# Scores one tile further ahead of the product with the values, and the queries split earlier, in a pooled-attention and maxout kernel

## The chip, the cores and the metric

The kernel runs on one core of a Trainium2 chip. The metric is the device time of one execution in microseconds. The engines are TensorE (PE in the profile, its weight loads PEld), VectorE (DVE), ScalarE (ACT), GpSimd (POOL) and SyncE (SP), which issues the DMAs.

## The reference

The keys and values are one tensor: a 4 x 4 mean of `kv` times a small matrix. The attention over 768 pooled positions is followed by a feed-forward part (FFN) with three matrices and a maximum.

```python
kv_pool = kv.reshape(B, H // r, r, W // r, r, C).mean(axis=(2, 4))      # r = 4
k = v = kv_pool.reshape(B, -1, C) @ w_sr                                # 4 x 768 x 128
s = scale * (q @ k.transpose(0, 2, 1))                                  # q: 4 x 12288 x 128
a = np.exp(s - s.max(-1, keepdims=True))
a /= a.sum(-1, keepdims=True) + 1e-09
x = (a @ v).reshape(B * N, C)
h = np.maximum(np.maximum(x @ w1, x @ w2), x @ w3)                      # 768 columns
return (h @ w_out).astype(np.float32)
```

## The kernel before

**Groups, tiles, steps.** The 49152 queries are worked through in 96 groups of 512 (24 to each batch). A group has four score tiles of 128 queries. The main loop at the end of the kernel runs over the groups g, and in each over six FFN steps f = 0 to 5, one for every 128 of the 768 hidden columns; n = 6 g + f counts them. While the FFN of group g runs, the scores of later groups, the product with the values of group g + 1, and the keys of the next batch are worked in between.

**The order.** What stands on each engine's queue is written out by hand: `ORDER` (L160) has twelve strings of tokens, the first six for the steps of an even group, the others for an odd one. `step` (L973) carries the tokens out one after the other, and every engine works its instructions in this order. The tokens that matter here:

- H: six matmuls into two banks ps_h (two buffers). R: ScalarE's Relu of the first bank. M: VectorE's h, the maximum of that with the second bank, which frees it.
- C: ScalarE's half-precision cast hh of h. L: GpSimd's remainder hl = h - hh. O: the product of the step two before with w_out, into ps_o; for f = 0 of a group it begins a new ps_o, of which there is one buffer.
- S: the six score matmuls of the next tile, into ps_s. m: VectorE's maximum mx and the bias nb. e: ScalarE's exponential a. c: ScalarE's cast ahl. l: GpSimd's remainder ahl, and a DMA that turns both halves into aT (two buffers, one per group).
- X: half of the product of aT with the values (ps_x) for group g + 1, at f = 1 and f = 4; for the first two groups both halves at f = 4. xh, xl: the halves of this product, at f = 5.
- P: VectorE copies the finished ps_o to o_planes, and a DMA turns it. G: VectorE's merge of what came back (o_sb<-o_turned). T: rs and the scaling (o_sb<-o_sb,w_down,rs), and the store.
- qd, qc, qp: once or twice per pair of groups, the load of 1024 queries, GpSimd's scaling of their columns, and VectorE's largest value with the scale q_up and q_sc. qh and ql: the two halves of 512 queries each; ScalarE casts q_hl from q_sb and q_up, VectorE makes the remainder q_hl, and a DMA turns both into qT (four buffers).
- k: a piece of the next batch's keys (`keys_step`, L1068). In groups 3 to 8 of a batch VectorE adds pieces of kv at f = 0, 2, 3 and 4 (odd groups) or sums them (even ones); groups 9 to 14 find the largest value, transpose and project.

**When a tile is scored.** Until group 1, `FIRST` says how many tiles S takes at each step; 13 are taken by its end, so it is one tile ahead of the three groups 1 to 3. From group 2 on S takes a tile at f = 0, 2, 3 and 5. So the last tile of group g + 2 is scored at f = 3 of group g, and X of that group begins at f = 1 of group g + 1. Between the score and its l lie two more steps: a tile scored at f = 3 is sent off by l at f = 0 of the next group, a tile scored at f = 2 at f = 4.

The queries of groups 2 p + 4 and 2 p + 5 are split (qh, ql) at f = 3 and f = 4 of the odd group 2 p + 1; ql stands behind M there.

Of the kernel before, what the change touches and what calls it, by code (L numbers as in the profile page):

```python
# [20 lines left out]
def kernel(  # L21
# [32 lines left out]
    B, N, C = q.shape  # L54
    _, HH, WW, _ = kv.shape
    R = 4
# [5 lines left out]
    NFT = DF // P  # L62
    G = 512
# [59 lines left out]
    def times(t, src, by, by2=None):  # L123
# [27 lines left out]
    FIRST = (1, 1, 2, 2, 0, 1, 1, 1, 1, 2, 0, 1)  # L151
    JOIN_ON_POOL, LO_ON_DVE, HI_ON_DVE, HL_ON_DVE = ((0, 2, 6), (3,), (6, 8), ())
    OUT_AT, OUT_ON = (1, 8), ("dve", "dve")
    ATTEND = {0: (4, 4), 1: (4, 4)}
    LATE = (1,)
    LOADS = (('k01', 'k00', 'k02', 'k03', 'q', 'k10', 'k11', 'k12', 'k13', 'k22', 'k20', 'k21', 'k23', 'w00', 'w10'), ('w20',), ('w01', 'w21', 'w11'))
    WEIGHTS = {(0, 0): (10, 12, 15, 18, 20, 21), (1, 0): (19, 20, 20, 20, 21, 21, 22), (2, 0): (21, 21, 21, 21, 21, 22, 22), (0, 1): (22, 22, 22, 23, 23, 23), (1, 1): (22, 23, 24, 24, 24, 24, 25), (2, 1): (24, 24, 25, 25, 25, 25, 25), (3, 0): (25, 25, 26, 26, 26, 26, 27), (3, 1): (26, 26, 26, 27, 27, 27, 27)}
    SIZE = {22: 0, 25: 1, 27: 2}
# [14 lines left out]
    )  # L173
    OUTS = {2: (), 3: (), 4: (0, 1, 2)}
# [141 lines left out]
    class Keys:  # L316
# [19 lines left out]
        def load(self, s, i):  # L336
            piece = kvp.tile([P, PIECE], F32, name="kv_piece")
            src = kv[self.b].rearrange("(s h i) (w r) c -> s i h w (r c)", s=KS, i=R, w=KW)
            sp_dma.dma_start(out=piece, in_=src[s, i])
            self.pieces[s, i] = piece  # L340
# [107 lines left out]
        def project(self, h):  # L448
            mm(
                out=self.spare()[:, :HALF], lhsT=wsr_sb, rhs=self.poolT[:, h * HALF:(h + 1) * HALF],  # L450
                start=True, stop=True,
            )
# [33 lines left out]
    def q_peak(s):  # L486

        assert s < 2 or next_q["cols"] >= 2 * s + 2
        row = qp.tile([P, 1], F32, name="q_row", bufs=2)
        dve.tensor_reduce(out=row, in_=st["q"][s], axis=AX.XY, op=ALU.max, apply_absolute_value=True)  # L490
        up = qp.tile([P, 1], F32, name="q_up", bufs=2)
        dve.tensor_scalar(
            out=row.bitcast(I32), in0=row.bitcast(I32), scalar1=EXPO, scalar2=None, op0=ALU.bitwise_and
        )
        dve.tensor_scalar(out=up, in0=row, scalar1=TINY, scalar2=2.0 ** -14, op0=ALU.max, op1=ALU.mult)
        dve.reciprocal(out=up, in_=up)
        st["qr"][s] = (row, up)
# [84 lines left out]
    def soft_max(g, j):  # L582
        mx = tiny.tile([P, 1], F32, name="mx")
        dve.tensor_reduce(out=mx, in_=st["ps"][g, j], axis=AX.XY, op=ALU.max, negate=True)
        soft_bias(g, j, mx)
# [76 lines left out]
    def hidden(g, f):  # L662
        xh, xl = st["x"][g]
        assert not st["hp"]
        fh, fs = f // (NFT // 2), slice(f % (NFT // 2) * P, (f % (NFT // 2) + 1) * P)
        for i in range(2):
            p = ps_h.tile([P, G], F32, name="ps_h")
            mm(out=p, lhsT=d_hi[i][fh][:, fs], rhs=xh, start=True, stop=False)
            mm(out=p, lhsT=d_lo[i][fh][:, fs], rhs=xh, start=False, stop=False)
            mm(out=p, lhsT=d_hi[i][fh][:, fs], rhs=xl, start=False, stop=True)  # L670
            st["hp"][i] = p

    def hidden_first():
        h1 = hp.tile([P, G], F32, name="h1", bufs=2)
        act.activation(out=h1, in_=st["hp"].pop(0), func=AF.Relu, scale=H_DOWN)
        return h1

    def hidden_max(h1):
        h = hp.tile([P, G], F32, name="h", bufs=4)
        dve.scalar_tensor_tensor(  # L680
            out=h, in0=st["hp"].pop(1), scalar=H_DOWN, in1=h1, op0=ALU.mult, op1=ALU.max
        )
        return h

    def hidden_hi(g, f):
        hh = hp.tile([P, G], F16, name="hh", bufs=HB_)
        act.copy(out=hh, in_=st["h"][g, f])
        st["h"][g, f] = (st["h"][g, f], hh)

    def hidden_lo(g, f):  # L690
        h, hh = st["h"][g, f]
        hl = hp.tile([P, G], F16, name="hl", bufs=HB_)
        (dve if g * NFT + f in HL_ON_DVE else pool).tensor_tensor(out=hl, in0=h, in1=hh, op=ALU.subtract)
        st["h"][g, f] = (hh, hl)
# [129 lines left out]
    k = KT[0] = Keys(0)  # L824
# [19 lines left out]
    def loads(n):  # L844
        for what in LOADS[n]:
            load(what)
# [98 lines left out]
    def late(n):  # L945
        if n == LATE[0]:
            q_peak(1)
            q_exps(1)
            q_split(2)
        weights(23 + n)  # L950
        if n in (1, 2):
            turn_w1(n - 1)
        if n == 5:
            product_w1()
# [14 lines left out]
    def drain(queue):  # L969
        while queue:  # L970
            yield queue.pop(0)

    def step(token, g, f):  # L973

        n = g * NFT + f
        if token == "H":
            hidden(g, f)
            to_relu.append((g, f))
        elif token == "R":
            for gf in drain(to_relu):  # L980
                to_h.append((gf, hidden_first()))
        elif token == "M":
            for gf, h1 in drain(to_h):
                st["h"][gf] = hidden_max(h1)
                to_hh.append(gf)
        elif token == "C":
            for gf in drain(to_hh):
                hidden_hi(*gf)
                to_hl.append(gf)
        elif token == "L":  # L990
            for gf in drain(to_hl):
                hidden_lo(*gf)
        elif token == "O":
            if g < 2:
                late(n)
            for m in OUTS.get(n, (n - 2,)):
                if m >= 0:
                    project(*divmod(m, NFT))
        elif token == "S":
            for _ in range(FIRST[n] if g < 2 else f not in (1, 4)):  # L1000
                if tiles:
                    to_max.append(tiles.pop(0))
                    scores(*to_max[-1])
        elif token == "X":
            for part, slot in enumerate(ATTEND.get(g, (1, 4))):
                if f == slot and g < NG - 1:
                    attend(g + 1, part)
        elif token == "m":
            for t in drain(to_max):
                soft_max(*t)  # L1010
                to_exp.append(t)
        elif token == "e":
            for t in drain(to_exp):
                soft_exp(*t)
                to_hi.append(t)
        elif token == "c":
            for t in drain(to_hi):
                soft_hi(*t)
                to_lo.append(t)
        elif token == "l":  # L1020
            for t in drain(to_lo):
                soft_lo(*t)
        elif token == "xh":
            if g + 1 < NG:
                attended_hi(g + 1)
        elif token == "xl":
            if g + 1 < NG:
                attended_lo(g + 1)
        elif token == "P":
            if g > 0:  # L1030
                turn_out(g - 1)
                to_merge.append((g - 1, n))
        elif token in ("G", "T"):
            if token == "G":
                while to_merge and (to_merge[0][1] < n - 1 or g == NG - 1 and f == NFT - 2):
                    m = to_merge.pop(0)[0]
                    merge(m)
                    to_scale.append(m)
            else:
                for m in drain(to_scale):  # L1040
                    scale_out(m, finish_scale(m))
        elif token == "qd":
            s = turn("load", NG // 2)
            if s:
                q_load(s)
        elif token == "qc":
            q = turn("cols", NG)
            if q:
                q_cols(q)
        elif token == "qp":  # L1050
            s = turn("peak", NG // 2)
            if s:
                q_peak(s)
                q_exps(s)
        elif token == "qh":
            q = turn("hi", NG)
            if q:
                q_hi(q)
        elif token == "ql":
            q = turn("lo", NG)  # L1060
            if q:
                q_lo(q)
        elif token == "k":
            keys_step(g, f)
        else:
            raise ValueError(token)
# [94 lines left out]
```

## Time and profile before

| | |
|---|---|
| time, median of 3 runs (lowest to highest) | 2059.89 us (2055.98 to 2059.9) |
| span of the profiled execution (its only time) | 2060.3 us |
| DVE q_hl, all of them | 96, 72.0 us |
| DVE h, all of them | 575, 396.5 us |
| DVE o_planes, all of them | 95, 115.9 us |
| POOL hl and ahl | 670.1 and 627.2 us |
| aT, median from issue to landing | 4.0 us |
| qT, median from issue to landing | 3.1 us |

An engine's share of busy time is over the whole span, of which the first 150 us are the start (weights, first keys). Matmuls overlap: each is drawn longer than the distance to the next one, so sums of their durations are larger than the time that they take. Nearly every line has the number of one helper, L103, so the groups are told apart by tiles. A row of the time line shows the start, the length, the engine, and what is written from what, and in brackets the idle time before it with what ended it.

### The profile page before, as it was taken

Reading aid. Unit: us, or ns where it says so; the run is one execution under the profiler, and the core shown is the slowest. Engines: PE = TensorE matmul, PEld = TensorE weight load, DVE = VectorE, ACT = ScalarE, POOL = GpSimd, SP = SyncE. Lnnn points to the kernel's source line nnn. Section 1 sums busy time; section 2 is a strip of 40 time slices with the busy share of each in tenths; the row PEclk is TensorE's granted clock in tenths of the full one; section 3 lists DMA queues with packets and bytes.
Section 4 is the critical chain, followed back from the end, with each engine's and each line's share of the span. In section 5 each row is a group of like instructions: output and inputs, shape, how many; then the busy total and the mean of one; then the engine's idle time right before and its main releaser. Section 6 shows DMA issues by size and latency. Waiting matters only on the chain.

```text
span 2060.3 us, 29166 instructions
## 1 busy us (share of the span) xinstructions
PE 1981.9 (96%) x9797; PEld 967.2 (47%) x9797; DVE 1510.4 (73%) x2482; ACT 1457.4 (71%) x2535; POOL 1409.2 (68%) x1064
## 2 busy tenths in 40 slices
PE   6489999999999999999999999999999999999998
PEld 5244444444444444444444444444444444444444
DVE  5767886677777887777777788677776777777775
ACT  2367777777777777777777777677777777777774
POOL 2257677777777767677776777677777776767764
PEclk8699999999999999999999999999999999999999
DMA  8177766667668876666667786757666676666662
GB/s 255 29 141 167 168 139 128 129 127 141 135 125 171 185 153 126 125 143 127 130 132 161 161 184 131 135 121 133 133 133 127 126 139 131 126 132 142 120 121 68
DMA packets 839959, 283.30 MB, mean 138 GB/s; under 512 B 813440, under 2 KB 814592, under 8 KB 839808
## 3 DMA queue, kind: packets, MB, share of 16 engines
q1 hardware_dynamic: 839808, 281.43, 66.5%
q8 instruction: 77, 1.26, 0.3%
q14 instruction: 74, 0.61, 0.1%
HBM read 53.54 MB, written 25.17 MB: 38 GB/s over the span
## 4 chain that ended last, share of the span: by engine, by line
PE 78%; DVE 8%; ACT 5%; DMA 5%; issue 2%; POOL 2%; SPq 0%; DVEq 0%; ACTq 0%; POOLq 0%
PE ps_h L103 30%; PE ps_o L103 17%; PE ps_x L103 16%; PE ps_s L103 15%; DMA aT<-ahl 4%; DVE h L103 1%; ACT ahl L103 1%; DVE kv_piece L103 1%; DVE q_row L103 1%; ACT a L103 1%; POOL ahl L103 1%; DVE mx L103 1%; ACT hh L103 1%; ACT xh L103 1%; ACT h L103 1%
## 5 line engine op out<-in xcount | busy, mean ns | idle before, releaser
L103 POOL TENSOR_TENSOR ahl<-a,ahl 128x768 f16<-128x768 f32 x383 | 627.2, 1648 | 321.9 <-issue 180.1
L103 POOL TENSOR_TENSOR hl<-h,hh 128x512 f16<-128x512 f32 x575 | 670.1, 1176 | 205.1 <-ACT hh L103 204.8
L103 DVE SCALAR_TENSOR_TENSOR h<-ps_h,h 128x512 f32<-128x512 f32 x575 | 396.5, 690 | 186.4 <-ACT h L103 90.5
L103 ACT ACTIVATE h<-ps_h 128x512 f32<-128x512 f32 x575 | 341.7, 594 | 243.7 <-PE ps_h L103 240.4
L103 ACT CAST hh<-h 128x512 f16<-128x512 f32 x577 | 349.8, 615 | 167.6 <-DVE h L103 167.4
L103 DVE TENSOR_REDUCE mx<-ps_s 128x1 f32<-128x768 f32 x383 | 365.4, 954 | 112.4 <-PE ps_s L103 111.9
L103 PE MATMUL ps_h<-xh,d_hi 128*128 128x512 f16 x1150 | 437.7, 381 | 7.6 <-ACT w1T L103 5.9
L103 PE MATMUL ps_h<-xh,d_lo 128*128 128x512 f16 x1150 | 437.7, 381 | 0.0
L103 PE MATMUL ps_h<-xl,d_hi 128*128 128x512 f16 x1150 | 437.6, 380 | 0.0
L103 ACT ACTIVATE a<-ps_s,nb,q_sc 128x768 f32<-128x768 f32 x383 | 377.4, 988 | 56.4 <-DVE nb L103 51.1
L103 PE MATMUL ps_x<-aT,v_hi 128*128 128x512 f16 (+1 forms) x1188 | 377.0, 376 | 22.5 <-DMA aT<-ahl 21.2
L103 PE MATMUL ps_s<-k_hi,qT 128*128 128x384 f16 x1532 | 376.3, 328 | 4.0 <-ACT a L103 3.3
L103 PEld LDWEIGHTS <-d_hi 128*128 128x128 f16 x2308 | 226.2, 98 | 258.8 <-issue 2.8
L103 PE MATMUL ps_o<-hh,wo 128*128 128x512 f16 x1140 | 340.5, 381 | 2.3 <-DVE wo L103 2.3
L103 PEld LDWEIGHTS <-qT 128*128 128x128 f16 x2304 | 226.7, 98 | 197.0 <-issue 10.1
L103 ACT CAST ahl<-a 128x768 f16<-128x768 f32 x382 | 312.4, 832 | 4.6 <-DMA aT<-ahl 0.2
L103 PEld LDWEIGHTS <-wo 128*128 128x128 f16 x1710 | 167.6, 98 | 195.1 <-DVE wo L103 2.3
L103 PE MATMUL ps_s<-k_lo,qT 128*128 128x384 f16 x766 | 251.5, 328 | 0.3 <-DVE k_lo L103 0.3
L103 PE MATMUL ps_x<-aT,v_lo 128*128 128x512 f16 (+1 forms) x594 | 222.7, 376 | 0.0
L103 PE MATMUL ps_o<-hl,wo 128*128 128x512 f16 x570 | 216.9, 380 | 0.0
L103 POOL TENSOR_TENSOR q_sb<-q_sb,col_row 128x512 f32<-128x512 f32 x96 | 126.2, 1315 | 101.4 <-DMA q_sb<-in_q_dram 91.4
L103 PEld LDWEIGHTS <-v_hi 128*128 128x128 f16 x1188 | 116.8, 99 | 149.7 <-DMA aT<-ahl 9.6
(148 smaller groups left out, 1425.8 us busy)
## 6 DMA issues: line engine op xcount, KB each, us to landing
kv_piece<-in_kv_dram SPq DMA_DIRECT2D x48, 512.0 KB, 5.0
q_sb<-in_q_dram SPq DMA_DIRECT2D x48, 512.0 KB, 4.5
out_dram<-o_sb SPq DMA_DIRECT2D x95, 256.0 KB, 2.2
aT<-ahl SPq DMA_TRANSPOSE x384, 4.0
kv_piece<-in_moe_w_dram SPq DMA_DIRECT2D x6, 384.0 KB, 5.6
qT<-q_hl SPq DMA_TRANSPOSE x96, 3.1
o_turned<-o_planes SPq DMA_TRANSPOSE x95, 3.3
kv_piece<-in_moe_w_out_dram SPq DMA_DIRECT2D x2, 384.0 KB, 3.8
```

Source lines behind the costliest of these rows:

```text
L103: return lambda **kw: tc.keep_in_program_order(op(**kw))
```

## The change

It adds one number and a condition: in group 2, S also takes a tile at f = 4 (n = 16). From then on every tile is scored one place earlier: the last tile of a group at f = 2 instead of f = 3, the first at f = 3 of the group before instead of f = 5. In the loop over S's places the tile that would have been taken last of all leaves its place empty. The tokens qh and ql leave f = 3 and f = 4 of the odd groups and come to f = 0 and f = 1; qh stands ahead of R, and ql behind M and behind k.

```diff
+    AHEAD = 2 * NFT + 4
...
     ORDER = (
...
-        "H C m l R M e k c L X O S",
-        "H C G R l L O m M c S k X e",
+        "H C m qh l R M e k c ql L X O S",
+        "H C G qh R l L O m M c S k ql X e",
         "H l P L k C R T e M m O S X c",
-        "H L C qh R m M l X O S e k ql c",
-        "H L m qh R l M c e X S O k C ql",
+        "H L C R m M l X O S e k c",
+        "H L m R l M c e X S O k C",
         "H xh m C L xl l c e R M O S X k qd",
     )
...
         elif token == "S":
-            for _ in range(FIRST[n] if g < 2 else f not in (1, 4)):
+            for _ in range(FIRST[n] if g < 2 else f not in (1, 4) or n == AHEAD):
```

On VectorE, in the odd group 69 from its maximum at f = 0 (the first row) to the h of f = 2 (the last), there stood before:

```order
L103 TENSOR_REDUCE mx<-ps_s 128x1
L103 TENSOR_SCALAR nb<-mx,q_sc 128x1
L103 SCALAR_TENSOR_TENSOR h<-ps_h,h_17048 128x512
L103 COPY o_sb<-o_turned 128x2x512
L103 TENSOR_REDUCE mx<-ps_s 128x1
L103 TENSOR_SCALAR nb<-mx,q_sc 128x1
L103 SCALAR_TENSOR_TENSOR h<-ps_h,h_17081 128x512
L103 COPY o_planes<-ps_o 128x1024
L103 TENSOR_SCALAR rs<-sm,o_down 128x4
L103 RECIPROCAL rs<-rs 128x4
L103 SCALAR_TENSOR_TENSOR o_sb<-o_sb,w_down,rs 128x512
L103 SCALAR_TENSOR_TENSOR h<-ps_h,h_17126 128x512
```

At the same place, from the h of f = 0 (the first row) on, there stands now:

```order
L103 SCALAR_TENSOR_TENSOR h<-ps_h,h_17069 128x512
L103 SCALAR_TENSOR_TENSOR q_hl<-q_sb,q_up,q_hl 128x4x128
L103 COPY o_sb<-o_turned 128x2x512
L103 TENSOR_REDUCE mx<-ps_s 128x1
L103 TENSOR_SCALAR nb<-mx,q_sc 128x1
L103 SCALAR_TENSOR_TENSOR h<-ps_h,h_17106 128x512
L103 SCALAR_TENSOR_TENSOR q_hl<-q_sb,q_up,q_hl 128x4x128
L103 COPY o_planes<-ps_o 128x1024
L103 TENSOR_SCALAR rs<-sm,o_down 128x4
L103 RECIPROCAL rs<-rs 128x4
L103 SCALAR_TENSOR_TENSOR o_sb<-o_sb,w_down,rs 128x512
L103 SCALAR_TENSOR_TENSOR h<-ps_h,h_17153 128x512
```

A q_hl has come behind each of the first two h, the second of them directly ahead of o_planes.

On ScalarE, from the cast hh at f = 0 of the same group (the first row) to the cast ahead of f = 2's Relu, there stood before:

```order
L103 CAST hh<-h 128x512
L103 ACTIVATE h_17048<-ps_h 128x512
L103 ACTIVATE a,sm<-ps_s,nb,q_sc 128x768
L103 CAST ahl<-a 128x768
L103 CAST hh<-h 128x512
L103 ACTIVATE h_17081<-ps_h 128x512
L103 ACTIVATE a,sm<-ps_s,nb,q_sc 128x768
L103 CAST hh<-h 128x512
```

And there stands now:

```order
L103 CAST hh<-h 128x512
L103 ACTIVATE q_hl<-q_sb,q_up 128x4x128
L103 ACTIVATE h_17069<-ps_h 128x512
L103 ACTIVATE a,sm<-ps_s,nb,q_sc 128x768
L103 CAST ahl<-a 128x768
L103 CAST hh<-h 128x512
L103 ACTIVATE q_hl<-q_sb,q_up 128x4x128
L103 ACTIVATE h_17106<-ps_h 128x512
L103 ACTIVATE a,sm<-ps_s,nb,q_sc 128x768
L103 CAST hh<-h 128x512
```

Each Relu (h from ps_h) of f = 0 and f = 1 now has a q_hl ahead of it. TensorE's queue differs in two places only: six score matmuls come in at step n = 16, and the last place of S, far down, is empty.

## The prediction

> **What bounds the kernel now.** I read the page's head first, then the table of stretches, then TensorE's waits after the start-up, which name what interrupts it.
>
> ```profile
> span 2060.3 us, 29166 instructions
> PE 1981.9 (96%) x9797; PEld 967.2 (47%) x9797; DVE 1510.4 (73%) x2482; ACT 1457.4 (71%) x2535; POOL 1409.2 (68%) x1064
> ```
>
> Stretches: length, then busy time of PE, PEld, DVE, ACT, POOL, and the granted clock.
>
> ```profile
> 400.00:600.00 200.00, 200.00 (x988) 96.43 (x987) 144.60 (x234) 148.95 (x259) 144.60 (x110) 1.00 0.67 133
> ```
>
> TensorE's waits from 150 us to the end: total us, times, longest.
>
> ```profile
> PE ps_x L103 <- DMA aT<-ahl: 12.6, 15, 2.3
> PE ps_x L103 <- DVE pool_max L103: 3.4, 3, 1.1
> PE ps_x L103 <- issue: 1.3, 2, 0.7
> ```
>
> TensorE bounds the steady part: 200.00 of 200 us busy at clock 1.00. The number of matmuls does not change, so only its waits can be won, and any new wait is lost in full. What is there to win is the product with the values (ps_x) waiting for the turned exponentials (aT), 12.6 us, and the two "issue" waits at the same product, 1.3 us.
>
> **What the change removes.** A recorded wait is short by a little. TensorE in order of time: start, length, instruction, [idle before it]:
>
> ```profile
> 151.66 0.39 PE L103 MATMUL ps_x<-aT,v_hi 128*128 128x512 f16 x1 [0.72 <-DMA aT<-ahl]
> ...
> 726.55 0.39 PE L103 MATMUL ps_x<-aT,v_hi 128*128 128x512 f16 x1 [1.81 <-DMA aT<-ahl]
> ...
> 1525.00 0.38 PE L103 MATMUL ps_h<-xh,d_hi 128*128 128x512 f16 x1
> 1525.22 0.38 PE L103 MATMUL ps_h<-xh,d_lo 128*128 128x512 f16 x1
> ...
> 1526.30 0.60 PE L103 MATMUL ps_o<-hh,wo 128*128 128x512 f16 x2
> ...
> 1527.92 0.38 PE L103 MATMUL ps_h<-xh,d_hi 128*128 128x512 f16 x1
> ```
>
> A matmul is drawn 0.38 us long, but its successor starts 0.22 us after it, so each wait costs 0.16 us more than is written. 17 waits make 13.9 + 17 x 0.16 = 16.6 us. One of them, 0.72 + 0.16 us at 151.66, belongs to group 3, whose tiles keep their places. So about **16 us** can go. I take all of it: the longest wait is 2.3 us, and a group's last tile is now split into halves and sent off two steps earlier (scored at f=2 and split at f=4, instead of f=3 and the next group's f=0); a step is 2.9 us (1525.00 to 1527.92) or more. The new overlap on the two aT buffers costs nothing: the first tile of group g+2 takes the buffer of group g, and ScalarE casts that tile behind the xh of group g, which itself waits for the product that frees the buffer. PE's only reordered instructions are one tile's six score matmuls at step 16, once: I cost them at nothing (one exponential is 0.99 us; up to that if they wait).
>
> **What the change moves.** Per pair of groups, two ScalarE casts (q_hl, hi) and two VectorE instructions (q_hl, lo) with their two transposes go from f=3 and f=4 of the odd group to f=0 and f=1. The transposes on SP go ahead of o_turned; each queued there follows its own producer, the SP queue is not what PE waits for, and qT is needed at f=3 only: nothing. What matters is VectorE. Here are the odd steps of a pair without key work (group 69): VectorE, then ScalarE, then GpSimd, in order of time.
>
> ```profile
> 1518.46 0.16 DVE L103 RECIPROCAL q_up<-q_up 128x1 f32<-128x1 f32 x1
> ...
> 1519.76 0.68 DVE L103 SCALAR_TENSOR_TENSOR h<-ps_h,h 128x512 f32<-128x512 f32 x1
> ...
> 1522.99 0.69 DVE L103 SCALAR_TENSOR_TENSOR h<-ps_h,h 128x512 f32<-128x512 f32 x1 [0.80 <-ACT h L103]
> 1523.60 1.22 DVE L103 COPY o_planes<-ps_o 128x1024 uint16<-128x1024 uint16 x1
> ...
> 1526.84 0.68 DVE L103 SCALAR_TENSOR_TENSOR h<-ps_h,h 128x512 f32<-128x512 f32 x1
> ```
>
> ```profile
> 1521.79 0.61 ACT L103 CAST hh<-h 128x512 f16<-128x512 f32 x1
> 1522.31 0.59 ACT L103 ACTIVATE h<-ps_h 128x512 f32<-128x512 f32 x1
> ...
> 1528.08 0.72 ACT L103 ACTIVATE q_hl<-q_sb,q_up 128x512 f16<-128x512 f32 x1
> 1528.77 0.60 ACT L103 ACTIVATE h<-ps_h 128x512 f32<-128x512 f32 x1
> ```
>
> ```profile
> 1523.62 2.28 POOL L103 TENSOR_TENSOR hl<-h,hh 128x512 f16<-128x512 f32 x2
> ```
>
> Step f=0: the first cast waits for q_up (1518.62), and its successor starts 0.69 us behind it (1528.08 to 1528.77), so the Relu h ends near 1519.97 and VectorE's h starts at 1520.06 instead of 1519.76. TensorE next writes that bank at 1521.1: hidden.
>
> Step f=1: the second cast takes the Relu's place at 1522.31; the Relu moves 0.69 us, and VectorE's h from 1522.99 to 1523.68 (the first q_hl and the merge o_sb fit into the 0.80 us in which VectorE waited). Then the second q_hl stands ahead of o_planes. It would start at 1524.28, and at that time GpSimd works on hl (1523.62 to 1524.78). What that means is shown by the same form of instruction elsewhere:
>
> ```profile
> 402.88 1.31 DVE L103 SCALAR_TENSOR_TENSOR o_sb<-o_sb,w_down,rs 128x512 f32<-128x512 f32 x1
> ...
> 1526.17 0.75 DVE L103 SCALAR_TENSOR_TENSOR o_sb<-o_sb,w_down,rs 128x512 f32<-128x512 f32 x1
> ```
>
> ```profile
> 402.45 1.20 POOL L103 TENSOR_TENSOR hl<-h,hh 128x512 f16<-128x512 f32 x1 [0.58 <-ACT hh L103]
> ```
>
> And VectorE's group of all q_hl: busy us, mean ns of one, then idle before:
>
> ```profile
> L103 DVE SCALAR_TENSOR_TENSOR q_hl<-q_sb,q_up,q_hl 128x512 f16<-128x512 f32 x96 | 72.0, 750 | 4.8 <-ACT q_hl L103 4.8
> ```
>
> Started inside a GpSimd instruction, o_sb took 1.31 us and ended 0.54 us after it (404.19 against 403.65); started outside, 0.75. The trace has no q_hl inside one: its mean of 750 ns over 96 is the undisturbed time. So its price here is between 0.74 us and, as o_sb paid, the end of hl plus 0.55: 1525.33. I take the latter, since the two have the same form and two SBUF inputs. o_planes then runs 1525.25 to 1526.47 instead of 1523.60 to 1524.82.
>
> The Trainium skill, page "SBUF — State Buffer", section "Who interferes with whom", says that a VectorE instruction with two SBUF inputs and a GpSimd instruction that reads SBUF exclude each other, and that whichever starts first holds the port for its whole length. The o_sb rows agree. By this rule the pair pays as I took it; were q_hl exempt, the pair would pay nothing.
>
> The product of step f=2 (ps_o, 1526.30) writes the bank that o_planes reads. How soon it follows is seen at the end of the run:
>
> ```profile
> 2042.15 1.23 DVE L103 COPY o_planes<-ps_o 128x1024 uint16<-128x1024 uint16 x1 [0.51 <-PE ps_o L103]
> ...
> 2043.43 0.38 PE L103 MATMUL ps_o<-w1o,xh 128*128 128x256 f16 x2
> ```
>
> 0.05 to 0.06 us behind. So it starts at 1526.53: **0.23 us** of TensorE per plain pair. The h behind it ends near 1528.3 and is needed at 1528.57 + 0.23: no second wait. Of 46 pairs that split q, 27 are plain: 6.2 us.
>
> **Pairs that add kv.** In nine pairs (groups 3, 5, 7 of 24, three key batches) VectorE also adds kv at f=0 and f=2. Group 27, GpSimd, VectorE and TensorE:
>
> ```profile
> 661.87 1.65 POOL L103 TENSOR_TENSOR ahl<-a,ahl 128x768 f16<-128x768 f32 x1 [2.33 <-issue]
> 663.48 2.80 POOL L103 TENSOR_TENSOR hl<-h,hh 128x512 f16<-128x512 f32 x2
> 667.15 1.67 POOL L103 TENSOR_TENSOR ahl<-a,ahl 128x768 f16<-128x768 f32 x1 [0.88 <-POOL hl L103]
> ...
> 664.58 0.68 DVE L103 TENSOR_TENSOR kv_piece<-kv_piece 128x512 f32<-128x512 f32 x1
> 665.18 1.13 DVE L103 TENSOR_SCALAR rs<-sm,o_down 128x4 f32<-128x4 f32 x1
> ...
> 667.23 0.68 DVE L103 SCALAR_TENSOR_TENSOR h<-ps_h,h 128x512 f32<-128x512 f32 x1
> ...
> 666.15 0.60 PE L103 MATMUL ps_o<-hh,wo 128*128 128x512 f16 x2
> ...
> 667.78 0.38 PE L103 MATMUL ps_h<-xh,d_hi 128*128 128x512 f16 x1
> ```
>
> The merge now falls at 661.76 to 662.5 and holds up ahl (661.87) by 0.46 us, so hl ends near 665.09, q_hl at 665.64, o_planes at 666.77: the product at 666.15 waits 0.68 us. Then the kv add ends near 667.36; ahl, due at 667.15, goes first and runs to 668.85; rs, and behind it o_sb, come after (as rs does here, 1.13 us instead of 0.28 beside hl). h ends near 670.5 instead of 667.91. TensorE needs its bank in the second half of the next step's matmuls, 667.78 + 0.65 + 0.68 = 669.1: 1.4 us more. Together 2.1 us a pair (bounds 0, if q_hl and o_sb slip in ahead of GpSimd, and 3.3, if ahl starts ahead of the merge), 18.9 us in nine. Nine more pairs have other key work at these steps (pool_max, pool_top, k_lo), shorter than a kv add: between the plain 0.23 and 2.1 us each; I take 0.7, nearer the plain row: 6 us. The first pair has no room at all:
>
> ```profile
> 127.94 1.22 DVE L103 COPY o_planes<-ps_o 128x1024 uint16<-128x1024 uint16 x1
> ...
> 129.21 0.59 PE L103 MATMUL ps_o<-hh,wo 128*128 128x512 f16 x2
> ```
>
> There the 1.65 us shift counts in full: 1.5 us (0 to 3).
>
> **Sum** against this execution's 2060.3 us (the median of the runs is 0.4 lower): -16.0 + 6.2 + 18.9 + 6.0 + 1.5 = +16.6, less 0.4: **2076.5 us**. At f=3 and f=4, which q leaves, nothing waited, so nothing comes back.
>
> **The rivals.**
> - *Not slower: the moved halves are hidden.* If the second q_hl does not wait for GpSimd, o_planes ends at 1526.17, 0.07 us ahead of need, and TensorE never waits. It decides at 1.4 us of lateness of o_planes. Then 2060.3 - 16.0 - 0.4 = 2044. For it: TensorE waits for none of these instructions today. Against: the shift of 1.65 us against a room of 1.42. Chance 0.18.
> - *Half and half.* The plain pairs escape by a tenth of a microsecond, the adding pairs pay only the late h, 1.4 us: -16 + 12.6 + 3 + 1.5, about 2061. Chance 0.16.
> - *GpSimd goes first at the merge* in the adding pairs: 3.3 us each, 11 us more: 2088. The margin is 0.11 us (661.76 against 661.87). Chance 0.07. The same section of the Trainium skill says that the order of issue, not the shape, decides who blocks; no row here shows which of the two starts first after the change.
> - *The change does not do what it says*: aT is late all the same, by the transposes that now share the queue. Then the 16 us stay beside part of the new waits: 2075 to 2093. The median landing of aT is 4.0 us against more than 5.8 us won, so 0.02.
> - The forecast, 2064 to 2088 by its bounds: 0.57.
>
> Some 0.2%, 4 us, is what a measurement of this kernel can tell from no change. Faster holds the first rival and a third of the second: 0.23. Within 0.2%: most of the rest of the second, 0.11. Slower: 0.66. The range is 2047 to 2088; it leaves out the clean gain and the far end of the third and fourth.
>
> **What would show it.** Right: ps_x no longer waits for aT beyond the first groups; ps_o waits for DVE o_planes some 40 times, mostly 0.2 us; ps_h waits for DVE h about ten times by over 1 us, all near kv adds; q_hl's mean rises from 750 ns towards 0.9 us. Wrong: ps_o never waits for o_planes, q_hl keeps 750 ns, or ps_x still waits for aT.

## The result, and the profile after

The changed kernel takes 2084.68 us (median of 4 runs, 2084.20 to 2084.85) beside 2059.80 us: the ratio is 1.0125, with a 95% interval of 1.0113 to 1.0137. It is slower by 25 us.

The head of its page, and TensorE's waits from 150 us to the end (total us, times, longest):

```profile
span 2082.4 us, 29145 instructions
PE 1990.3 (96%) x9797; PEld 968.7 (47%) x9797; DVE 1520.6 (73%) x2482; ACT 1465.9 (70%) x2535; POOL 1422.2 (68%) x1064
```

```profile
PE ps_h L103 <- DVE h L103: 19.4, 19, 1.8
PE ps_o L103 <- DVE o_planes L103: 8.1, 14, 1.0
PE ps_x L103 <- DVE pool_max L103: 3.4, 3, 1.1
```

The shares of busy time are what they were, and the number of matmuls too. The waits have changed: those of ps_x for aT and for "issue" (13.9 us in their rows before) are gone, and only those for pool_max are as they were. In their place TensorE waits for VectorE: at the banks of the hidden columns (ps_h for h) and at the output's bank (ps_o for o_planes). Each such wait costs 0.16 us more than its row says, and some 30 of ps_o are shorter than that and have no row at all.

A pair without key work shows these short ones. VectorE, GpSimd and TensorE at f = 1 and f = 2 of group 69, in order of time:

```profile
1546.33 0.69 DVE L103 SCALAR_TENSOR_TENSOR h<-ps_h,h 128x512 f32<-128x512 f32 x1 [0.56 <-ACT h L103]
1546.93 1.11 DVE L103 SCALAR_TENSOR_TENSOR q_hl<-q_sb,q_up,q_hl 128x512 f16<-128x512 f32 x1
1547.97 1.21 DVE L103 COPY o_planes<-ps_o 128x1024 uint16<-128x1024 uint16 x1
...
1549.63 0.75 DVE L103 SCALAR_TENSOR_TENSOR o_sb<-o_sb,w_down,rs 128x512 f32<-128x512 f32 x1
```

```profile
1546.34 1.16 POOL L103 TENSOR_TENSOR hl<-h,hh 128x512 f16<-128x512 f32 x1
```

```profile
1548.81 0.38 PE L103 MATMUL ps_h<-xl,d_hi 128*128 128x512 f16 x1
1549.24 0.38 PE L103 MATMUL ps_o<-hh,wo 128*128 128x512 f16 x1
```

In this pair the second q_hl starts inside GpSimd's hl (1546.34 to 1547.50), takes 1.11 us and ends 0.54 us behind it; o_planes ends at 1549.18, and the product, due at 1548.81 + 0.22 = 1549.03, starts at 1549.24. That is 0.21 us, with nothing written beside it.

A pair that adds kv, group 27, the same engines:

```profile
670.26 0.74 DVE L103 COPY o_sb<-o_turned 128x1024 uint16<-128x1024 uint16 x1
...
672.65 1.48 DVE L103 SCALAR_TENSOR_TENSOR q_hl<-q_sb,q_up,q_hl 128x512 f16<-128x512 f32 x1
674.05 1.21 DVE L103 COPY o_planes<-ps_o 128x1024 uint16<-128x1024 uint16 x1
675.18 0.68 DVE L103 TENSOR_TENSOR kv_piece<-kv_piece 128x512 f32<-128x512 f32 x1
675.78 1.62 DVE L103 TENSOR_SCALAR rs<-sm,o_down 128x4 f32<-128x4 f32 x1
...
678.32 0.68 DVE L103 SCALAR_TENSOR_TENSOR h<-ps_h,h 128x512 f32<-128x512 f32 x1
```

```profile
670.46 2.01 POOL L103 TENSOR_TENSOR ahl<-a,ahl 128x768 f16<-128x768 f32 x1 [2.33 <-issue]
...
675.74 1.64 POOL L103 TENSOR_TENSOR ahl<-a,ahl 128x768 f16<-128x768 f32 x1 [0.59 <-POOL hl L103]
```

```profile
675.32 0.38 PE L103 MATMUL ps_o<-hh,wo 128*128 128x512 f16 x1 [0.42 <-DVE o_planes L103]
...
679.05 0.38 PE L103 MATMUL ps_h<-xh,d_hi 128*128 128x512 f16 x1 [1.31 <-DVE h L103]
```

Here the merge (o_sb<-o_turned) has held up ahl (2.01 us, not 1.65), hl and q_hl are late, and TensorE waits 0.42 + 0.16 us for o_planes. Then rs waits out the next ahl (675.74 to 677.38), o_sb and h come behind it, and TensorE waits another 1.31 + 0.16 us.

Counted from start to start of the matmuls (by how much one starts later than 0.22 us behind the one before it, or 0.16 us behind one of 384 columns), from 123 us on and without waits under 0.15 us, the waits of both traces are:

| us (times) | before | after |
|---|---|---|
| ps_x for aT, and "issue" there | 18.0 (18) | 0.6 (1) |
| ps_o for o_planes | 0.3 (2) | 18.4 (44) |
| ps_h for h | 0.3 (1) | 22.5 (19) |

17.4 us won and 40.3 us lost are 22.9 us; the spans differ by 22.1 us. The medians differ by 2.8 us more. Of the runs whose span is listed, each takes 1.8 us more than it, so the profiled execution of before, with 2060.3 us, was one of the longer ones of its kernel.

### The profile page after: what moved, and what is told of

Same layout as the page of the kernel before. It is cut to its first block, busy times and chain, and to the rows that moved or that the text cites. A ratio compares the mean times of both kernels' runs of the same rounds, so it can differ in the third digit from the quotient of the medians.

```text
span 2082.4 us, 29145 instructions
## 1 busy us (share of the span) xinstructions
PE 1990.3 (96%) x9797; PEld 968.7 (47%) x9797; DVE 1520.6 (73%) x2482; ACT 1465.9 (70%) x2535; POOL 1422.2 (68%) x1064
## 5 line engine op out<-in xcount | busy, mean ns | idle before, releaser
L103 POOL TENSOR_TENSOR ahl<-a,ahl 128x768 f16<-128x768 f32 x383 | 637.8, 1675 | 294.5 <-issue 176.4
L103 DVE SCALAR_TENSOR_TENSOR xl<-ps_x,xh 128x512 f16<-128x512 f32 x96 | 66.4, 692 | 189.0 <-ACT xh L103 189.0
L103 PEld LDWEIGHTS <-d_lo 128*128 128x128 f16 x1154 | 113.0, 98 | 150.2 <-issue 33.8
```

Of the source, the lines that this page charges most:

```text
L103: return lambda **kw: tc.keep_in_program_order(op(**kw))
```

## The experiments

Times are medians, each with its ratio to the kernel before, run on the same chip. The waits are in us, counted as above, in each run's profiled execution.

| run | us | ratio (95%) | aT | o_planes | h |
|---|---|---|---|---|---|
| before | 2059.80 | | 18.0 | 0.3 | 0.3 |
| changed kernel | 2084.68 | 1.0125 (1.0113 to 1.0137) | 0.6 | 18.4 | 22.5 |
| e1: halves moved, no tile ahead | 2082.95 | 1.0106 (1.0092 to 1.0120) | 3.4 | 15.4 | 20.1 |
| e2: tile ahead, first half only | 2063.60 | 1.0016 (1.0007 to 1.0025) | 1.7 | 2.1 | 16.5 |
| e10: e2 without the tile ahead | 2071.20 | 1.0050 (1.0032 to 1.0068) | 13.4 | 1.6 | 12.0 |
| e3: second half with one input | 2069.01 | 1.0040 (1.0026 to 1.0053) | 0.9 | 5.6 | 20.1 |
| e4: second half behind o_planes | 2098.05 | 1.0178 (1.0164 to 1.0192) | 0.7 | 2.6 | 38.1 |
| e7: changed kernel, h ahead of rs | 2078.94 | 1.0089 (1.0069 to 1.0110) | 0.4 | 18.4 | 9.6 |
| e8: e2, h ahead of rs | 2079.88 | 1.0091 (1.0074 to 1.0108) | 1.9 | 2.1 | 20.0 |
| e9: second half only | 2115.98 | 1.0269 (1.0252 to 1.0286) | 2.6 | 26.3 | 42.8 |
| e5: tile ahead, q work off these steps | 2050.23 | 0.9952 (0.9940 to 0.9965) | 3.5 | 0.2 | 1.6 |
| e6: e5 without the tile ahead | 2107.11 | 1.0232 (1.0218 to 1.0246) | 62.2 | 0.2 | 0 |

**e1. The halves alone.** The changed kernel without the extra tile:

```diff
-            for _ in range(FIRST[n] if g < 2 else f not in (1, 4) or n == AHEAD):
+            for _ in range(FIRST[n] if g < 2 else f not in (1, 4)):
```

> The queries' halves stand at f=0 and f=1 as in the changed kernel, but group 2 takes no extra tile, so every tile keeps its old place. Theory: the moved halves alone make VectorE late, and the tile further ahead alone removes the waits for aT; the two parts add. Then the new waits of the changed kernel (about 17 us of ps_o for o_planes, about 22 us of ps_h for h, from start to start) stand beside the old 17 us for aT: 2059.8 + 39 = 2099 us, at the least 2090. Rival 1: the tile further ahead is what costs (buffers of aT, order of the exponentials): 2060. Rival 2: the new waits swallow the old ones, since a TensorE that is held up waits less for aT: 2082 to 2086, with less than 4 us for aT.

TensorE's waits from 150 us on:

```profile
PE ps_h L103 <- DVE h L103: 17.3, 17, 1.4
PE ps_o L103 <- DVE o_planes L103: 5.4, 9, 1.0
...
PE ps_x L103 <- DMA aT<-ahl: 1.3, 3, 0.5
PE ps_x L103 <- issue: 0.6, 1, 0.6
```

2083.0 us, nearly that of the changed kernel: the second rival was right, the theory's sum of 2099 was not. The moved halves make the kernel slow by themselves. They also take away most of the waits for aT, from 18.0 to 3.4 us, without any tile further ahead. That a TensorE which is held up at f = 2 of the odd group comes later to the next product, when aT has landed, fits this; no run shows it pair by pair.

**e2 and e10. The first half alone,** with and without the extra tile. The second half is back at f = 4:

```diff
-        "H C G qh R l L O m M c S k ql X e",
+        "H C G R l L O m M c S k X e",
...
-        "H L m R l M c e X S O k C",
+        "H L m qh R l M c e X S O k C ql",
```

> The tile further ahead stays, the first half stays at f=0, and the second half goes back to f=4 of the odd group. Theory: the first half fits into the time in which VectorE waited for the Relu, and only the second one pushes o_planes. Then the waits of ps_o for o_planes and of ps_h for h go but for some in the pairs that add kv (0 to 4 us in all), aT is not waited for: 2043 to 2049 us, faster than both. Rival (the first half costs as much as the second): about 2064 to 2066. Rival (the tile further ahead costs): 2075 or more.

> As e2 (first half at f=0, second at f=4 of the odd group), without the extra tile in group 2. Theory: the 16.5 us of ps_h waits stay, and they swallow the aT waits of the pairs that add kv, which are most of the 17 us; what is left of aT is 3 to 8 us: 2065 to 2072 us. Rival (the tile further ahead is worth its full 16 us whatever else waits): 2077 to 2081 us. Rival (worth nothing): 2062 to 2064.5 us.

In e2, VectorE and GpSimd at f = 2 of group 27:

```profile
667.57 2.23 DVE L103 SCALAR_TENSOR_TENSOR o_sb<-o_sb,w_down,rs 128x512 f32<-128x512 f32 x1
669.72 0.68 DVE L103 SCALAR_TENSOR_TENSOR h<-ps_h,h 128x512 f32<-128x512 f32 x1
```

```profile
667.61 1.64 POOL L103 TENSOR_TENSOR ahl<-a,ahl 128x768 f16<-128x768 f32 x1 [0.32 <-POOL hl L103]
```

e2 missed its expectation of 2043 to 2049 us: 2063.6. In plain pairs nothing waits, as expected. But in each of the nine pairs that add kv the first half alone brings VectorE so far behind that o_sb waits until ahl has ended (2.23 us in group 27, not 0.75), and h makes TensorE wait, 1.57 us in eight of them. The second half is the difference to the changed kernel, 21 us. e10 came at 2071.2 us, within its range, but not by its sum: 13.4 of the 18.0 us of waits for aT are left, not 3 to 8, and the h waits did not stay at 16.5 us but fell to 12.0. Beside the first half the extra tile is worth 7.6 us (7 by the ratios, since the two ran on different chips).

**e3. What the second q_hl waits for.** It reads one input instead of two:

```diff
+        if g > 4 and g % 2:
+            dve.tensor_reduce(out=hl[:, :, 1], in_=t.unsqueeze(3), axis=AX.X, op=ALU.max)
```

> The changed kernel, but the second half's VectorE instruction is a reduction over an axis of one, which reads one input from SBUF in place of two; it leaves out the remainder of the second half of the queries (a value of q stands in its place). Theory: the wait of q_hl for GpSimd's hl is what makes o_planes late in plain pairs. Then all q_hl of this kind take 0.7 to 0.8 us, o_planes ends 0.3 to 0.4 us earlier in plain pairs and 0.7 us earlier in those that add kv; the 0.2 us of the plain pairs go, and the waits of the others shrink: 2066 to 2078 us. Rival (the shift of the Relu and the bare length of q_hl are enough): 2083 to 2086.

The groups of q_hl on VectorE (busy us, mean ns), first in the changed kernel, then in e3, where the second half's are the 46 reductions:

```profile
L103 DVE SCALAR_TENSOR_TENSOR q_hl<-q_sb,q_up,q_hl 128x512 f16<-128x512 f32 x96 | 91.5, 953 | 4.8 <-ACT q_hl L103 4.8
```

```profile
L103 DVE SCALAR_TENSOR_TENSOR q_hl<-q_sb,q_up,q_hl 128x512 f16<-128x512 f32 x50 | 37.1, 743 | 4.8 <-ACT q_hl L103 4.8
L103 DVE TENSOR_REDUCE q_hl<-q_sb 128x512 f16<-128x512 f32 x46 | 31.1, 676 | 0.0
```

2069.0 us, within the theory's range: the waits for o_planes fall from 18.4 to 5.6 us with the instruction at the same place in the queue. In plain pairs none is left: o_planes ends 0.28 us ahead of the product (group 69), and the reduction is only 0.07 us shorter than an undisturbed q_hl (676 against 743 ns). So it is the waiting behind GpSimd, not the bare length of q_hl and not the shift of the Relu, that makes o_planes late there, and in eight of the nine pairs that add kv. What is left is in the first pair, in group 3 and in the three pairs in which k_lo is made. The h waits hardly change (22.5 to 20.1): o_sb still comes too late for its turn.

**e4. The second half behind o_planes.**

```diff
-        "H C G qh R l L O m M c S k ql X e",
-        "H l P L k C R T e M m O S X c",
+        "H C G qh R l L O m M c S k X e",
+        "H l P ql L k C R T e M m O S X c",
```

> The changed kernel, but the second half's remainder (and its transposed copy) stands behind o_planes at f=2 instead of ahead of it. Theory: ps_o then never waits for o_planes (at most 0.1 us in the first pairs), but q_hl meets the next hl of GpSimd, and what is behind it (rs, o_sb, h) comes 0.6 to 1.2 us later: the ps_h waits for h grow, in plain pairs from 0 to something between 0.1 and 1.5 us. In all 2050 to 2110 us, ps_o under 2 us, ps_h over 22 us. Rival (a bare 0.7 us of VectorE, without a wait for GpSimd): ps_h hardly waits in plain pairs, 2050 to 2060 us.

o_planes is freed (2.6 us left) and h pays (38.1 us, 21 rows, up to 2.9 us): the lateness is passed on to what is behind. But it is so almost only in pairs with key work. In plain pairs q_hl does wait behind hl (1.43 us in group 69), and TensorE then waits for h by 0.05 us in 25 of 27, less than the theory's 0.1 to 1.5 (1.57 us in the other two).

The waits of the table make 23 us, and the span is 35.5 us longer than before. The rest is the clock. Of the thirteen h waits over 2 us, seven are followed within 1 us by a stretch of 3.4 us at half clock (granted 0.50); one begins 0.4 us after this wait (the second line gives length, busy time and number of PE, PEld, DVE, ACT and POOL, then the clock 0.50):

```profile
1230.75 0.38 PE L103 MATMUL ps_h<-xh,d_hi 128*128 128x512 f16 x1 [2.09 <-DVE h L103]
```

```profile
1231.15:1234.55 3.40, 3.40 (x11) 1.40 (x10) 1.91 (x4) 2.61 (x5) 1.72 (x2) 0.50 0.96 218
```

Seven times 3.4 us at 0.50 lose 12 us. No other trace here has such a stretch between 123 us and its last 10 us, and why six of the thirteen waits are not followed by one stays open.

**e7 and e8. h ahead of rs and the scaling,** in the changed kernel and in e2:

```diff
-        "H l P L k C R T e M m O S X c",
+        "H l P L k C R M T e m O S X c",
```

> The changed kernel, but at f=2 of the odd groups VectorE's h stands ahead of rs and the scaling o_sb, not behind them. Theory: the ps_h waits for h of the changed kernel (22 us, 19 times) are rs and o_sb waiting for GpSimd's ahl in front of h; they go, and the ps_o waits for o_planes (18 us) stay: 2062 to 2067 us. Rival (VectorE is short of time in these steps, whatever the order): the waits move to ps_s, ps_h a step later or aT, 2078 us or more.

> As e2 (first half at f=0, second at f=4, tile further ahead), with h ahead of rs and the scaling at f=2 of the odd groups. Theory: of the 16.5 us of ps_h waits that e2 kept, the ones of 1.57 us in the pairs that add kv go: 2046 to 2050 us. Rival (VectorE short of time): 2058 us or more.

Both missed the theory's times. TensorE's waits in e8:

```profile
PE ps_h L103 <- DVE h L103: 15.6, 23, 1.7
...
PE ps_o L103 <- POOL hl L103: 4.7, 13, 0.5
```

In e7 the h waits do fall, from 22.5 to 9.6 us, and the traced execution is 12.5 us shorter (2069.9 against 2082.4); but its other runs took 2078.1 to 2082.4 us beside the traced one's 2071.8, and why they differ stays open. In e8 the h waits do not go, and new ones come, 11.9 us from start to start for GpSimd's hl: rs and o_sb, now later, meet other GpSimd instructions (in group 15 rs takes 1.76 us behind an ahl and o_sb 1.39 behind an hl). There the order of two instructions has moved the waits and not removed them.

**e5 and e6. The queries' work off these steps,** with and without the extra tile. The scales (qp) go to f = 4 and the first half to f = 5 of the even group, the second half back to f = 4 of the odd one:

```diff
-        "H L S C m l R M O c e X k",
-        "H m C xh l xl R c e M L S O qp k X",
-        "H C m qh l R M e k c ql L X O S",
-        "H C G qh R l L O m M c S k ql X e",
+        "H L S C m l R M O c e X qp k",
+        "H m C xh l xl R c e M L qh ql S O k X",
+        "H C m l R M e k c L X O S",
+        "H C G R l L O m M c S k X e",
...
-        "H L m R l M c e X S O k C",
+        "H L m qh R l M c e X S O k C ql",
```

> The tile further ahead, but the queries' work leaves the full steps: the largest value and scales (qp) go from f=5 to f=4 of the even group, the first half from f=0 to f=5, the second half back to f=4 of the odd group. Theory: the tile further ahead is worth about 16 us where nothing makes VectorE late between f=0 and f=2 of the odd group. Then ps_h waits for h under 3 us, ps_o for o_planes under 2 us, aT under 2 us: 2042 to 2048 us. Rival: the tile further ahead brings nothing of its own, since another wait always takes the place of aT: 2058 to 2063 us.

> As the last one, without the extra tile in group 2. Theory: the waits for aT are back, 12 to 18 us from start to start, and nothing else: 2056 to 2062 us. Rival (the earlier scales and halves are what gains): 2042 to 2050 us.

TensorE's waits in e5, then in e6:

```profile
PE ps_x L103 <- DVE pool_max L103: 4.6, 3, 1.5
PE ps_x L103 <- DMA aT<-ahl: 1.8, 1, 1.8
PE ps_x L103 <- issue: 1.4, 1, 1.4
PE ps_h L103 <- DVE h L103: 1.4, 1, 1.4
```

```profile
PE ps_x L103 <- DMA aT<-ahl: 44.8, 46, 1.5
PE ps_x L103 <- issue: 7.0, 7, 1.2
```

e5 takes 2050.2 us, 0.5% less than the kernel before, and beats both; it is 2 us over its expected range. What it still waits for aT is in groups 3 and 4, ahead of the extra tile's effect. e6 missed by far: 2107 us and 62 us of waits for aT. Where TensorE waits for aT there, it is 44.8 / 46 + 0.16 = 1.1 us each time. What delays the tiles is seen in the trace of e6. GpSimd, VectorE and SyncE's queue ahead of the product of group 69:

```profile
1547.98 1.64 POOL L103 TENSOR_TENSOR ahl<-a,ahl 128x768 f16<-128x768 f32 x1 [0.80 <-POOL hl L103]
```

```profile
1548.51 1.67 DVE L103 SCALAR_TENSOR_TENSOR q_hl<-q_sb,q_up,q_hl 128x512 f16<-128x512 f32 x1 [0.54 <-ACT q_hl L103]
```

```profile
1550.20 1.23 SPq L103 DMA_TRANSPOSE qT<-q_hl  x1
1551.53 1.47 SPq L103 DMA_TRANSPOSE aT<-ahl  x1
```

ahl is done at 1549.62, but its transpose stands behind that of q_hl, which waits for VectorE until 1550.18: it is issued 1.9 us late (0.03 us at this place before) and lands at 1555.20, and the product starts at 1555.25. In e5 the same transpose is issued just as late (1.9 us), and no product waits for it: one place further ahead, the tile sent off here is already the first of the next group. No run takes this one transpose out of the way by itself. What the runs do show: the extra tile is worth 57 us here, 7.6 us beside the first half of e2, and nothing beside both halves (2084.7 against 2083.0). No run has the extra tile with both halves left where they stood before, so its worth alone stays open.

**e9. The second half alone:** e5 with the second half at f = 1 of the odd group, as in the changed kernel.

> The tile further ahead, scales at f=4 and first half at f=5 of the even group as in e5, but the second half at f=1 of the odd group as in the changed kernel. Theory: each half has its own waits. The second half's Relu shift and its wait behind GpSimd's hl give the ps_o waits for o_planes (plain pairs 0.2 us; 8 to 18 us in all), and the lateness that they leave makes o_sb miss its turn before ahl in the pairs that add kv (9 x 1.3 us of ps_h and more): 2070 to 2080 us. Rival (the two halves only hurt together): 2050 to 2056 us.

VectorE in a plain pair, from the first half on:

```profile
1556.28 1.67 DVE L103 SCALAR_TENSOR_TENSOR q_hl<-q_sb,q_up,q_hl 128x512 f16<-128x512 f32 x1 [0.54 <-ACT q_hl L103]
...
1566.12 2.19 DVE L103 SCALAR_TENSOR_TENSOR o_sb<-o_sb,w_down,rs 128x512 f32<-128x512 f32 x1
1568.23 0.68 DVE L103 SCALAR_TENSOR_TENSOR h<-ps_h,h 128x512 f32<-128x512 f32 x1
```

It missed: 2116 us, more than with both halves at f = 0 and f = 1. Now even in plain pairs o_sb loses its turn to ahl, and TensorE waits 0.61 us for o_planes and 0.96 us for h in nearly each. The two halves do not have prices that add; where each falls among GpSimd's instructions decides.

## Why the prediction was right

The forecast was 2076.5 us by new waits of 32.6 us against 16.0 us won. By its steps:

- **aT, -16.0 us.** The waits went: 17.4 us. The cause given holds only in part. e1 shows that the moved halves alone take away 14.6 of the 18.0 us, so the extra tile added almost nothing to this result. The sum took the two for independent, which they are not; that this term came out all the same was luck.
- **Plain pairs, 0.23 us each.** 0.21 us, by the chain that was worked out: q_hl ends 0.54 us behind hl, o_planes behind it. e3 took the wait away, and the waits for o_planes fell by 12.8 us.
- **Pairs that add kv, 2.1 us each.** 0.42 + 1.31 + 2 x 0.16 = 2.05 us in group 27 and in seven more, with rs behind ahl as forecast. In group 3 the merge itself started behind ahl, the third rival's case, and the pair cost 3.8 us (forecast for it: 3.3). In all 20.2 us.
- **Nine more pairs with key work, 6 us.** This term was mis-sized: 12.7 us. The three with pool_top cost nothing, the three with pool_max 1.6 us each, and the three in which k_lo is made 2.7 us each. In those last three the merge started behind ahl; that is the third rival's mechanism, which had been weighed for the kv pairs alone. VectorE there in group 13, the merge first, and GpSimd's ahl:

```profile
384.71 2.19 DVE L103 COPY o_sb<-o_turned 128x1024 uint16<-128x1024 uint16 x1
...
389.15 1.22 DVE L103 COPY o_planes<-ps_o 128x1024 uint16<-128x1024 uint16 x1
...
391.17 2.03 DVE L103 SCALAR_TENSOR_TENSOR o_sb<-o_sb,w_down,rs 128x512 f32<-128x512 f32 x1
```

```profile
384.33 1.96 POOL L103 TENSOR_TENSOR ahl<-a,ahl 128x768 f16<-128x768 f32 x1 [2.65 <-issue]
```

- **First pair, 1.5 us.** 1.53 us from start to start, against 0.16 before.
- **From the span to the time, -0.4 us.** Runs take 1.8 us more than their span, and the traced execution of before was one of its kernel's longer ones, at 2060.3 us: that is 2.8 us of the 8.2 us that the forecast was short.
- **"Fits into the 0.80 us"**, said of the first half, is right in plain pairs only. e2 shows 16.5 us of h waits from the first half alone, all in pairs with key work, and the signs had put the long waits for h near kv adds only: of the 14 over 1 us from start to start, five are in pairs with pool_max and k_lo.

Of the rivals, the hidden one asked that q_hl not wait for GpSimd; it did, 953 ns in the mean instead of 750. (One of the 96 had waited before too: 1.38 us at 137.47, inside an ahl.) The Trainium skill's rule in "SBUF — State Buffer", section "Who interferes with whom", is borne out for q_hl by e3: with two inputs it waited, with one it did not.

## What to carry to other kernels

Where one engine is busy throughout, look for what an instruction moved on another engine will run beside, not only for whether that engine has time: two VectorE instructions of 0.7 us each were free at f = 3 and f = 4 and cost up to 3.8 us in a pair at f = 0 and f = 1, because there they met GpSimd. Waits on one bottleneck replace one another, so the price of a wait that is removed is found with the other change in place and without it; here the same tile of look-ahead was worth 0, 7.6 and 57 us. When an added load makes a step late, try other places for it, each with the gain in place: one of them turned 1.0125 into 0.9952, another (e9) made it 1.0269.

## What was not expected of the hardware

The start shown in the profile does not settle whose turn it is. In e2 o_sb started 0.04 us ahead of GpSimd's ahl (667.57 against 667.61) and still ended 0.55 us behind it, at 669.80; in the changed kernel's plain pairs, with 0.39 us ahead (1549.63 against an ahl at 1550.02), it took its 0.75 us, and so it did in e4 with 0.08 us ahead (1565.57 against 1565.65; there ahl took 2.17 us). So two engines with fixed programs can lose 1.5 us in pair after pair by less than a tenth of a microsecond, and a margin as narrow as this cannot be read off the starts.
